# Accumulating the seven products of a Strassen-like group in shared PSUM banks, on one Trainium2 core

## The chip, the core and the metric

The kernel runs on one core of a Trainium2 chip. The engines of the core are named as the profile names them: PE does matrix products (PEld is its loading of weights, which runs beside PE), DVE and ACT are the vector and the scalar engine, POOL and SP mostly issue DMAs here. Each engine works through its own queue in program order and waits on semaphores for the others. Matrix products are written to PSUM, whose banks hold 128 partitions x 512 fp32 values here; DVE and ACT read them there, and DMA moves data between device memory and SBUF. The metric is the device time of one execution in microseconds (us), as the median of several runs.

## The reference

The input `x` has 2048 tokens of 576 channels. The result is `x` plus two branches of the normalised input `xn`: a sliding-window dilated attention (window 8, dilation 2) with its projections, and a mixer with an MLP. The change lies in the MLP:

```python
xn = _layernorm(x, axis=-1)
return x + _A_ref(xn, A_wqkv, A_wo) + _B_ref(xn, B_w1, B_w2, B_w3, B_w4)
...
# in _B_ref, with x1 the result of the token mixing, D = 576, F = 4608
h2 = _gelu(_layernorm(x1, axis=-1) @ w3) @ w4
return x1 + h2
```

All of it is fp32. The kernel reaches that by splitting each operand into a rounded part (fp32r) and a remainder, and multiplying the parts.

## The kernel before

The 4608 hidden columns of the MLP are taken 128 at a time. The first 24 such blocks (12 pairs, `NPL = 12`) go through a plain path: `up` computes a block of `x1 @ w3` for 512 tokens in one PSUM bank, ACT applies the Gelu straight from the bank (`gelu_ps`, lines 783 and 784), `low_part` (line 794) makes the remainder on DVE, and `down` (line 819) multiplies with `w4`.

The last 12 blocks go through the stage that is changed here. It takes a pair of blocks and two blocks of 512 tokens as a 2 x 2 block product, and computes that with seven products of combined operands in place of eight (the Winograd form of Strassen's scheme). A turn of this is a group; there are `NQ = 12` of them, `q = 0` to 11, six for each half of the tokens. The combined operands A11, A12, A22, S1 to S4 (from `w3`) and B11, B21, B22, T1 to T4 (from the tokens) lie ready in SBUF, with signs folded in.

- A product (`product`, line 1056) is seven matmuls (`HALVES`) that accumulate in one bank of 128 x 512 fp32. The banks are named `cc0` to `cc3` and are taken in turn by a count, `nps[1] % 4`. Each of the seven products of a group takes the next.
- The seven products are combined on the way out. ACT copies P1 from its bank into the SBUF buffer Z1 (line 1234). DVE adds the banks of the other six to such buffers (`z_add`, line 1060), P5's bank twice: seven additions a group. They leave c11 in Z4, c22 in Z1, c21 in Z3 and c12 in Z2.
- The Gelu of each of these four is a pair of ACT instructions that read the buffer in SBUF (`gelu_z`, lines 789 and 790): one writes the rounded result to the tile `h`, the other writes the full result back into the buffer. `low_part` then makes the remainder.
- D0 to D7 are eight down projections (`down`), twelve matmuls each, of the hidden values of the group before. Their results go either through ACT (`act.copy` at line 823 into a staging buffer, and a DMA by POOL that adds to device memory, line 824) for the tiles listed in `YD`, or are added to Y by DVE (line 827). Two pairs of banks take turns for them. Of D4 to D7, the last three go through ACT.

The order of the products and down projections of a group is written out by hand: `ORDER = "P1 P2 P6 P5 P7 D0 P4 D1 P3 D2 D3 D4 D5 D6 D7"`, with other orders for groups 0, 1, 5 and 6 (`ORDERS`). In group 6 it begins with `D0 D1 P1 P2`. A `plan` hangs further work behind each of these steps: the splitting of weights (`split_a`, `split_s`, `split_w4`, whose ACT part is line 562) and of token operands (`split_op`, lines 876 to 878 on ACT, after D5 of groups 2 and 3 among others), the combination of weights on DVE (`combine`), DMA loads, and the Gelus of c22 (`gelu22`) and c12 (`gelu12`, at D5 in most groups). The Gelu of c11 follows P5. The Gelu of c21 stands at the start of the next group's code, ahead of its P1, so that on ACT it comes behind the copy of D7. On every engine the instructions stand in the order in which this code issues them.

## Time and profile before

| | |
|---|---|
| timed runs (3) | median 1285.24 us, 1284.25 to 1286.41 |
| span of the profiled execution | 1285.6 us |
| stage with the seven products | about 925 to 1198 us of the span |
| groups, products, down projections in it | 12, 84, 96 |
| PE, DVE, ACT busy in it | 272.6, 202.5 and 146.8 of 273 us |

The profile has of the profiled execution its span; the time that lies around the span isn't shown in it. How to read its lines: in a timeline, the first number is the start in us from the start of the span, the second the busy time in us, then engine, line of the kernel, operation, output `<-` input and shape; brackets hold the idle time of that engine just ahead of the instruction and what ended it. In a list of groups, `x84 | 56.4, 686 | 31.5 <-PE cc L1056 30.9` means 84 instructions, 56.4 us in all, 686 ns each, and 31.5 us idle before them, of which 30.9 ended with that line of PE. In a list of waits, the numbers are the total in us, how often, and the longest.

### The profile page before, as it was taken

What the parts mean: (1) busy time and instruction counts of PE and PEld (TensorE: products, weight loads), DVE (VectorE), ACT (ScalarE), POOL (GpSimd) and SP (SyncE); (2) the same over time, 40 slices, a digit from 0 to 9 for tenths busy, and PEclk for the clock granted to TensorE, in tenths of its full rate; (3) what the DMA queues carried; (4) which work ended last, traced back from release to release, by engine and by line L of the source; (5) the groups of instructions that cost most, each with busy time, mean ns of one, the idle gap of its engine ahead of it and who ended that gap; (6) DMA issues with size and microseconds to landing.
All of it is one profiled execution on the core that took longest, in us unless ns stands there. A gap on an engine that the chain in (4) does not pass through costs nothing.

```text
span 1285.6 us, 19627 instructions
## 1 busy us (share of the span) xinstructions
PE 1271.5 (99%) x7594; PEld 1169.7 (91%) x7594; DVE 950.8 (74%) x1355; ACT 547.0 (43%) x876; POOL 214.3 (17%) x318
## 2 busy tenths in 40 slices
PE   8999999999999999999999999999999999999998
PEld 8999998899898999898989999998899998999998
DVE  6455534677568899999999999967777766887541
ACT  3332125525634434343434343433846567355530
POOL 2011100021221221221211221111112112112200
PEclk9999999999999999999999999999999999999999
DMA  7646784246896887987776867467847787788972
GB/s 205 156 121 138 168 175 140 82 113 194 194 268 147 171 158 200 191 169 151 172 162 144 181 134 164 79 125 179 196 86 128 161 185 150 168 203 188 263 251 83
DMA packets 196173, 210.22 MB, mean 164 GB/s; under 512 B 77920, under 2 KB 134176, under 8 KB 195952
## 3 DMA queue, kind: packets, MB, share of 16 engines
q1 hardware_dynamic: 165536, 144.82, 38.7%
q0 software_dynamic: 30544, 64.16, 31.7%
q8 instruction: 59, 0.97, 0.3%
q14 instruction: 34, 0.28, 0.1%
HBM read 112.98 MB, written 107.28 MB: 171 GB/s over the span
## 4 chain that ended last, share of the span: by engine, by line
PE 78%; issue 7%; DMA 6%; DVE 5%; ACT 2%; POOL 1%; SPq 1%; POOLq 0%; DVEq 0%; ACTq 0%
PE ps L819 26%; PE p L800 21%; PE ps L212 16%; PE cc L1056 6%; PE ps L462 4%; PE ps L309 3%; POOL yd L824 1%; DMA xn<-st 1%; DMA x1n<-xn 1%; DVE L L729 1%; PE ps L477 1%; DMA yd<-ev 1%; SPq L579 1%; DMA yd<-Y 1%; DMA xt<-xn 1%
## 5 line engine op out<-in xcount | busy, mean ns | idle before, releaser
L819 PEld LDWEIGHTS ps<-w,c 128*128 128x128 f32 x3456 | 466.6, 188 | 14.6 <-DVE Y L827 4.0
L819 PE MATMUL ps<-w,c 128*128 128x288 f32 x3456 | 473.1, 294 | 5.6 <-DVE Y L827 2.8
L824 POOL DMA_DIRECT2D yd<-Y x125 | 109.2, 876 | 449.0 <-ACT Y L823 407.7
L823 ACT COPY Y<-ps 128x576 f32<-128x576 f32 x125 | 79.9, 640 | 168.9 <-PE ps L819 86.6
L794 DVE TENSOR_TENSOR c<-Y,c 128x512 fp32r<-128x512 f32 x144 | 98.9, 687 | 59.1 <-ACT Y L784 45.9
L783 ACT ACTIVATE c<-p 128x512 fp32r<-128x512 f32 x96 | 57.6, 600 | 188.9 <-PE p L800 188.9
L212 PE MATMUL ps<-WQ,xt 128*128 128x432 f32 x672 | 134.8, 360 | 0.0
L212 PEld LDWEIGHTS ps<-WQ,xt 128*128 128x128 f32 x672 | 125.6, 188 | 5.7
L726 DVE TENSOR_TENSOR prod<-q,k 128x1152 f32<-128x1152 f32 x64 | 86.6, 1353 | 10.1 <-DMA k<-qkvd 9.4
L827 DVE TENSOR_TENSOR Y<-ps,Y 128x576 f32<-128x576 f32 x108 | 81.2, 752 | 13.5 <-PE ps L819 13.3
L729 DVE TENSOR_REDUCE L<-prod 128x64 f32<-128x1152 f32 x64 | 86.4, 1351 | 1.1
L824 POOL DMA_DIRECT2D yd<-ev x55 | 47.8, 888 | 214.3 <-ACT ev L823 213.2
L800 PE MATMUL p<-xt,w3a 128*128 128x512 f32 x336 | 78.9, 391 | 1.3 <-ACT Y L784 1.3
L1060 DVE TENSOR_TENSOR Y<-cc,Y 128x512 f32<-128x512 f32 x84 | 56.4, 686 | 31.5 <-PE cc L1056 30.9
L800 PE MATMUL p<-xt,w3s 128*128 128x512 f32 x336 | 78.5, 390 | 0.0
L800 PE MATMUL p<-x1n,w3s 128*128 128x512 f32 x336 | 78.5, 390 | 0.0
L800 PE MATMUL p<-x1n,w3a 128*128 128x512 f32 x336 | 78.5, 390 | 0.0
L705 DVE TENSOR_TENSOR prod<-v,L 128x1152 f32<-128x1152 f32 x56 | 75.8, 1354 | 0.8
L709 DVE TENSOR_TENSOR o<-o,prod 128x1152 f32<-128x1152 f32 x56 | 75.8, 1353 | 0.6
L800 PEld LDWEIGHTS p<-xt,w3a 128*128 128x128 f32 x336 | 62.2, 188 | 14.8 <-ACT Y L784 2.1
L119 POOL TENSOR_TENSOR rs<-rs,mhalf 128x1 f32<-128x1 f32 x48 | 30.9, 645 | 261.0 <-DVE rs L118 148.3
L800 PEld LDWEIGHTS p<-xt,w3s 128*128 128x128 f32 x336 | 62.4, 188 | 12.6
(194 smaller groups left out, 1782.1 us busy)
## 6 DMA issues: line engine op xcount, KB each, us to landing
yd<-Y POOLq DMA_DIRECT2D x127, 288.0 KB, 5.3
yd<-ev POOLq DMA_DIRECT2D x55, 288.0 KB, 5.1
Y<-in_B_w_dram SPq DMA_DIRECT2D x23, 576.0 KB, 6.0
w3st<-in_B_w_dram SPq DMA_DIRECT2D x44, 256.0 KB, 6.0
qkvd<-stg SPq DMA_DIRECT2D x24, 432.0 KB, 3.5
xd<-st SPq DMA_DIRECT2D x16, 320.0 KB, 6.0
xd<-big SPq DMA_DIRECT2D x16, 320.0 KB, 7.1
xin<-in_A_x_dram SPq DMA_DIRECT2D x16, 288.0 KB, 3.8
```

Of the source, the lines that this page charges most:

```text
L212: pe.matmul(ps[:, h, :n], xs(a), ws(b, h), start=i == 0, stop=i == len(PAIRS) - 1)
L705: dve.tensor_tensor(dst, vv, Lf[:, :, w:w + 1].to_broadcast([128, TPP * GH, HD]), op=ALU.mult)
L709: dve.tensor_tensor(o, o, dst, op=ALU.add)
L726: dve.tensor_tensor(prod.rearrange("p (j h) d -> p j (h d)", h=GH), q, k[:, r0:r0 + TPP, :], op=ALU.mult)
L729: dve.tensor_reduce(Lf[:, :, w], prod, axis=AX.X, op=ALU.add)
L794: dve.tensor_tensor(h[:, 1, :], g, h[:, 0, :].bitcast(F32), op=ALU.subtract)
L800: pe.matmul(ps, W3[f][:, w, :], x1n[b][:, a, :], start=n == 0, stop=n == len(PAIRS) - 1)
L819: pe.matmul(ps[:, k, :HF], h[:, col], w[:, p, k * HF:(k + 1) * HF], start=n == 0, stop=n == len(seq) - 1)
L823: act.copy(e.rearrange("p (h c) -> p h c", h=2), ps[:, :, :HF])
L824: pool.dma_start(yd[t], e, accum_op=ALU.add)
L827: dve.tensor_tensor(yv, ps[:, :, :HF], yv, op=ALU.add)
L1056: pe.matmul(ps, WX[w][:k, v, SLOT[w], :], area[sb][xk][:k, a, :], start=i == 0, stop=i == len(HALVES) - 1)
```

## The change

Four of the seven products of a group (P1, P6, P7, P4) accumulate in one bank, `ca`, and two (P5, P3) in another, `cc`; P2 has a bank of its own, `cb`. After P1, after P6 and after P7 ACT copies the sum so far from `ca` into Z1, Z2 and Z3 (`keep`). DVE adds P2's bank to Z1, giving c11; P5's bank to Z3, giving c22; and, after P3, the bank with P5 and P3 to Z2, giving c12. With P4 the bank `ca` holds c21, and its Gelu reads it there (`gelu_ps`), writing the full result to Z4. So a group takes three banks in turn where it took seven. Where the sums lie in SBUF changes with it: c11 in Z1, c22 in Z3. `gelu_ps` and `z_add` are not changed.

```diff
-    def product(w, xk):
-        nps[1] += 1
-        ps = qpc.tile([128, 512], F32, name=f"cc{nps[1] % 4}")
+    def product(w, xk, onto=None, last=False):
+        ps = onto
+        if ps is None:
+            nps[1] += 1
+            ps = qpc.tile([128, 512], F32, name=f"cc{nps[1] % 4}")
         for i, (a, v) in enumerate(HALVES):
             k = 128 if a else 96
-            pe.matmul(ps, WX[w][:k, v, SLOT[w], :], area[sb][xk][:k, a, :], start=i == 0, stop=i == len(HALVES) - 1)
+            pe.matmul(ps, WX[w][:k, v, SLOT[w], :], area[sb][xk][:k, a, :],
+                      start=onto is None and i == 0, stop=last and i == len(HALVES) - 1,
+                      skip_group_check=True)
         return ps
+
+    def keep(z, ps):
+        act.copy(by_token(z), in_order(ps))
...
         if q:
-            h21 = gelu_z("c21", Z3)
+            h21 = gelu_ps("c21", ca, Z4)
...
-            hid[q, "c22"] = gelu_z("c22", Z1)
+            hid[q, "c22"] = gelu_z("c22", Z3)
...
-        low22 = lambda: low_part(hid[q, "c22"], Z1)
+        low22 = lambda: low_part(hid[q, "c22"], Z3)
...
             if it == "P1":
-                c1 = product("A11", "B11")
-                act.copy(by_token(Z1), in_order(c1))
+                ca = product("A11", "B11")
+                keep(Z1, ca)
                 if q:
-                    low_part(h21, Z3)
+                    low_part(h21, Z4)
             elif it == "P2":
-                c2 = product("A12", "B21")
-                z_add(Z4, c2, Z1)
+                cb = product("A12", "B21", None, True)
+                z_add(Z1, cb, Z1)
             elif it == "P6":
-                c6 = product("S2", "T2")
-                z_add(Z2, c6, Z1)
+                product("S2", "T2", ca)
+                keep(Z2, ca)
             elif it == "P5":
-                c5 = product("S1", "T1")
-                h11 = hid[q, "c11"] = gelu_z("c11", Z4)
+                cc = product("S1", "T1")
+                h11 = hid[q, "c11"] = gelu_z("c11", Z1)
             elif it == "P7":
-                c7 = product("S3", "T3")
-                z_add(Z3, c7, Z2)
-                z_add(Z1, c5, Z3)
-                z_add(Z2, c5, Z2)
-                low_part(h11, Z4)
+                product("S3", "T3", ca)
+                keep(Z3, ca)
+                z_add(Z3, cc, Z3)
+                low_part(h11, Z1)
             elif it == "P4":
-                c4 = product("A22", "T4")
-                z_add(Z3, c4, Z3)
+                product("A22", "T4", ca, True)
             elif it == "P3":
-                c3 = product("S4", "B22")
-                z_add(Z2, c3, Z2)
+                product("S4", "B22", cc, True)
+                z_add(Z2, cc, Z2)
...
-    h21 = gelu_z("c21", Z3)
+    h21 = gelu_ps("c21", ca, Z4)
...
-            low_part(h21, Z3)
+            low_part(h21, Z4)
```

## The prediction

> **What bounds the kernel now.** I read the page's busy shares first, then the stage that holds all the edits, then the matrix engine's waits in it, and last the two engines that gain and lose work, in order of time.

> ```profile
> span 1285.6 us, 19627 instructions
> PE 1271.5 (99%) x7594; PEld 1169.7 (91%) x7594; DVE 950.8 (74%) x1355; ACT 547.0 (43%) x876; POOL 214.3 (17%) x318
> 925.00:1198.00 273.00, 272.64 (x1622) 247.22 (x1621) 202.48 (x340) 146.84 (x230) 46.91 (x55) 1.00 0.75 163
> PE ps L819 <- ACT ev L823: 0.4, 1, 0.4
> ```

> The third line is one stretch of the busy-time-by-stretches view: the seven-product stage, 273 us of twelve groups, with the busy time of PE, PEld, DVE, ACT and POOL, then the granted clock (1.00). The fourth is the whole list of PE's waits in that stretch: a single one of 0.4 us. So in this stage PE alone sets the time, DVE is idle a quarter of it and ACT almost half. An edit can gain at most about that one gap (0.4 us, and below 1 us with its restart); it can lose as much as it makes PE wait.

> One group in PE's timeline (start, busy us, instructions):

> ```profile
> 1111.85 3.40 PE L1056 MATMUL cc<-x1n,w3a 128*128 128x512 f32 x14
> 1115.09 3.39 PE L1056 MATMUL cc<-xt,w3s 128*128 128x512 f32 x14
> 1118.31 1.77 PE L1056 MATMUL cc<-x1n,w3s 128*128 128x512 f32 x7
> 1119.92 1.75 PE L819 MATMUL ps<-w,c 128*128 128x288 f32 x12
> 1121.51 1.78 PE L1056 MATMUL cc<-xt,w3a 128*128 128x512 f32 x7
> ```

> P1 and P2 stand in the first row, P6 and P5 in the second, then P7, D0 and P4. From start to start a product takes (1115.09 - 1111.85) / 2 = 1.62 us and a down projection 1.59 us. A row's busy time runs some 0.16 us past the next row's start, because matmuls overlap.

> **What the change removes and adds, off the path.** The matmuls are the same in number and shape and PE's order of products and downs is unchanged; no DMA is added, removed or moved on any queue.

> ```profile
> L1060 DVE TENSOR_TENSOR Y<-cc,Y 128x512 f32<-128x512 f32 x84 | 56.4, 686 | 31.5 <-PE cc L1056 30.9
> L1234 ACT COPY Y<-cc 128x512 f32<-128x512 f32 x12 | 6.8, 570 | 1.0 <-PE cc L1056 1.0
> ```

> DVE loses four of seven additions a group: 12 x 4 x 0.686 = 33 us of its 202. ACT gains two copies a group: 12 x 2 x 0.570 = 14 us on its 147. Both still lie under PE's 273, and PE never waited for DVE here, so the 33 us are worth nothing.

> **New waits inside a group.** P6, P7 and P4 now write the bank that ACT has just copied out, so each must wait for the copy before it. The second copy, for one, starts about 0.1 us after P6's last matmul, which ends 1.78 us after P6 starts; with 0.57 us and 0.05 us of signalling P7 is free 2.5 us after P6's start, and PE wants it only at 2 x 1.62 = 3.24, since P5 stands between. P4 has D0 between: 1.62 + 1.59 = 3.21 against 2.5. P3 writes onto the bank that DVE reads after the third copy: 2.5 + 0.1 + 0.69 = 3.3 against 6.4 from P7's start, or 4.8 in the groups with fewer downs between. Cover is 0.7 us where it is thinnest; without it the loss would be 0.19 us and more each time (restart, below). The Gelus that read the sums get them no later than before: c11 still after P2's addition, c22 after a copy and one addition where it had two additions, c12 after P3's. All this holds where ACT is not late, and in the middle of a group it has holes (first row, 7.55 us). Only in group 0 it is late, behind operand splits (second and third row):

> ```profile
> 1124.93 0.64 ACT L823 COPY ev<-ps 128x576 f32<-128x576 f32 x1 [7.55 <-PE ps L819]
> 929.29 0.58 ACT L1234 COPY Y<-cc 128x512 f32<-128x512 f32 x1
> 929.96 3.40 PE L1056 MATMUL cc<-xt,w3s 128*128 128x512 f32 x14
> ```

> The copy ends at 929.87 and P6 starts at 929.96, its weight load a little earlier: I book 0.15 us, bounds 0 and 0.3.

> **The new wait at the boundary of groups.** Here is the cost. Seven banks a group were taken in turn from four; now three are. Group g takes the counts 3g+1 (four products), 3g+2 (P2) and 3g+3; the next group's P2 takes 3g+5, which modulo 4 is 3g+1: the bank in which group g's c21 stands. Formerly c21 was finished into SBUF by DVE and its Gelu read that; now the Gelu pair reads the bank itself, and it stands in ACT's queue where it always stood, behind D7's copy. So P2 must wait for the end of that pair, and all of PE's queue with it; nobody then waits for P2 but work that itself has slack. ACT at the same boundary:

> ```profile
> 1108.88 0.64 ACT L823 COPY ev<-ps 128x576 f32<-128x576 f32 x1 [1.34 <-PE ps L819]
> 1111.14 1.16 ACT L562 CAST w<-Y 128x1152 fp32r<-128x1152 f32 x1
> 1112.19 0.64 ACT L823 COPY ev<-ps 128x576 f32<-128x576 f32 x1
> 1112.72 0.64 ACT L789 ACTIVATE c<-Y 128x512 fp32r<-128x512 f32 x1
> 1113.40 0.63 ACT L790 ACTIVATE Y<-Y 128x512 f32<-128x512 f32 x1
> 1113.93 0.57 ACT L1234 COPY Y<-cc 128x512 f32<-128x512 f32 x1
> ```

> D5's copy waited for PE (1.34 us), then ACT is busy without a hole: Gelu of c12, D6's copy, the w4 cast, D7's copy, and at 1112.72 and 1113.40 the pair in question. P2 would start at 1111.85 + 1.62 = 1113.47, before the pair's end. How long the pair takes from a PSUM bank shows in the stage before, where the same two activations read one:

> ```profile
> 902.65 0.60 ACT L783 ACTIVATE c<-p 128x512 fp32r<-128x512 f32 x1 [2.53 <-PE p L800]
> 903.14 0.59 ACT L784 ACTIVATE Y<-p 128x512 f32<-128x512 f32 x1
> ```

> 1.08 us from the first start to the second end, against 1.31 above from SBUF. So P2 is released at 1112.72 + 1.08 + 0.05 = 1113.85, 0.38 us late. [...]

> Two boundaries, into groups 3 and 4, have an operand split (three activations) in ACT's chain after D5:

> ```profile
> 1013.56 1.04 ACT L876 ACTIVATE xt<-xt 128x1024 fp32r<-128x1024 f32 x1
> 1015.82 0.62 ACT L823 COPY ev<-ps 128x576 f32<-128x576 f32 x1
> 1017.92 0.64 ACT L789 ACTIVATE c<-Y 128x512 fp32r<-128x512 f32 x1
> 1014.80 3.40 PE L1056 MATMUL cc<-x1n,w3a 128*128 128x512 f32 x14
> 993.93 0.64 ACT L789 ACTIVATE c<-Y 128x512 fp32r<-128x512 f32 x1
> 990.81 3.40 PE L1056 MATMUL cc<-x1n,w3a 128*128 128x512 f32 x14
> ```

> The split pushes D6's copy out by 1015.82 - 1013.56 = 2.26 us. P2 is wanted at 1014.80 + 1.62 = 1016.42 and released at 1017.92 + 1.13 = 1019.05: 2.63 us late. The other one: 993.93 + 1.13 - 992.43 = 2.63.

> Of the other eight (into groups 1, 2, 5, 7 to 11) the first and the last:

> ```profile
> 943.54 0.63 ACT L789 ACTIVATE c<-Y 128x512 fp32r<-128x512 f32 x1
> 942.80 3.40 PE L1056 MATMUL cc<-x1n,w3a 128*128 128x512 f32 x14
> 1184.79 0.64 ACT L789 ACTIVATE c<-Y 128x512 fp32r<-128x512 f32 x1
> 1183.91 3.40 PE L1056 MATMUL cc<-x1n,w3a 128*128 128x512 f32 x14
> ```

> 944.67 against 944.42 is 0.25, 1185.92 against 1185.53 is 0.39. Done the same way, the eight are 0.25 twice and 0.37 to 0.39 six times: 2.8 us. Into group 6 there is none: two downs stand between the pair and P1.

> **What a stop costs beside its length.** The one wait of this kind that the stage has:

> ```profile
> 1061.32 0.62 ACT L823 COPY ev<-ps 128x576 f32<-128x576 f32 x1
> 1061.99 4.92 PEld L819 LDWEIGHTS ps<-w,c 128*128 128x128 f32 x36 [0.59 <-ACT ev L823]
> 1061.99 5.16 PE L819 MATMUL ps<-w,c 128*128 128x288 f32 x36 [0.36 <-ACT ev L823]
> 1066.99 3.39 PE L1056 MATMUL cc<-x1n,w3a 128*128 128x512 f32 x14
> 1083.07 4.92 PE L819 MATMUL ps<-w,c 128*128 128x288 f32 x36
> 1087.83 3.40 PE L1056 MATMUL cc<-x1n,w3a 128*128 128x512 f32 x14
> ```

> The copy ends at 1061.94 and PE goes on at 1061.99 (the 0.05 used above), but its three downs take 1066.99 - 1061.99 = 5.00 us, against 1087.83 - 1083.07 = 4.76 without a stop. The weight load, too, restarts only at the release, and is no longer under a matmul. Lower bound 0, upper 0.24; I take 0.19 (the page has 188 ns for a load), ten times: 1.9 us. [...] The row has the load waiting.

> **Sum.** 2 x 2.63 + 2.8 + 1.9 + 0.15 = 10.1 us. PE is saturated, so none of it is made up later, and ACT's chain at each boundary is tied to D5's end on PE, so the lateness repeats unchanged. The profiled span of 1285.6 lies 0.4 us above the median of the timed runs, 1285.24; the span would be 1295.7, and the time 1285.24 + 10.1 = 1295.3.

> **The rivals.**
> Not slower: DVE's 33 us bring ACT's chain forward, so the pair ends before P2 wants the bank. Then P2 costs nothing and at best the stage's one gap goes: 1285.24 - 0.6 (0.36 idle, 0.24 restart) = 1284.6. It decides once the pair ends 0.6 us earlier at eight boundaries and 2.8 at two. For it: ACT does wait for DVE's additions in places.

> ```profile
> L789 ACT ACTIVATE c<-Y 128x512 fp32r<-128x512 f32 x48 | 30.4, 634 | 15.1 <-DVE Y L1060 15.1
> 1214.13 1.85 PE L819 MATMUL ps<-w,c 128*128 128x288 f32 x12 [1.28 <-ACT Y L823]
> ```

> The first row has these 15.1 us. Against: the chain that sets the pair starts from PE's D5, not from DVE. 5%.
> Only the long stalls: the short ones (0.25 to 0.39 us) vanish if ACT runs a little tighter, as with a copy less at the boundary. 2 x (2.63 + 0.19) = 5.6, so 1290.9. Against: six instructions in a row there have no hole. 9%.
> Later gaps swallow part: the 0.6 us gap at 1061.99 and the 1.28 us one at 1214.13 (row above) close if their cause, DMA landings say, does not shift with PE: 1295.3 - 1.9 = 1293.4. Against: the first hangs on ACT work behind D1's copy, which shifts too. 8%.
> Weight loads run ahead: the load under a waiting matmul is done by the time it is released, so a stop costs its length alone, 10.1 - 1.9 = 8.2 and 1293.4. For it: loads do overlap matmuls everywhere else. Against: PEld's row at 1061.99, and the 5.00 us for three downs. 10%. [...]
> The in-group waits bite: if waiting products lose the weight load's cover even where the copy is in time, 36 waits x 0.19 = 6.8 more: 1302.1. Against: PE's rows show an even 1.62 us although products waited for older readers of their banks before. 8%.

> **How the numbers follow.** The forecast has 60%. Its own range: restarts 0 to 0.24 (8.2 to 10.6), pair 0.1 us shorter or longer at ten boundaries (1 us), so 1292.5 to 1297. The range is widened to the cheaper rivals and part of the way to the dearer one: 1290.5 to 1299. About 0.2% (2.6 us) is what a measurement can tell from no change. Only the first rival is not slower: 2% faster, 4% the same, 94% slower; the point over its 5% is for causes that I don't see.

> **What would show it.** PE's waits in the stage should list P2 (the products' line) waiting for the second Gelu, ten times, two of them near 2.5 us, with the weight load waiting alongside; DVE busy about 33 us less, ACT about 11 to 14 us more; P6, P7, P4 and P3 with no waits except perhaps group 0. I would be wrong if P1 and P2 stay 1.62 us apart at the boundaries, if the copies appear among PE's waits, or if PE's granted clock falls after the long stalls.

## The result and the profile after

The median of five runs is 1297.14 us (1294.95 to 1300.15), against 1286.41 us (1284.25 to 1287.11, five runs) for the kernel before, measured beside it: a ratio of 1.0091 [1.0078, 1.0104], slower by 10.7 us. Ratios here and below are estimated from the single runs, with a 95% interval; the quotient of two medians differs a little (1.0083 here). The profiled execution took 1297.46 us, its span is 10.1 us longer than before's.

The page of the kernel after (its span and busy shares), then the row of the seven-product stage in the busy-time-by-stretches view (length, then PE, PEld, DVE, ACT, POOL busy, then the granted clock):

```profile
span 1295.7 us, 19586 instructions
PE 1274.2 (98%) x7594; PEld 1168.2 (90%) x7594; DVE 921.3 (71%) x1307; ACT 558.4 (43%) x900; POOL 214.4 (17%) x318
925.00:1208.00 283.00, 276.17 (x1624) 246.58 (x1623) 173.45 (x293) 158.02 (x254) 47.43 (x55) 1.00 0.74 157
```

DVE has 48 instructions and 29.5 us less, ACT 24 instructions and 11.4 us more, PE the same 7594 matmuls. DVE was relieved as intended, and the kernel got slower: the stage is 10 us longer, and PE, busy for 272.6 of 273 us before, now is for 276.2 of 283. The granted clock is 1.00 in both. So the new time is time in which PE stands.

The kernel after: PE's waits in the stage, then those of its weight loads (what waits, for what, total us, times, longest):

```profile
PE cc L1058 <- ACT Y L784: 6.3, 8, 2.5
PE ps L819 <- ACT ev L823: 0.4, 1, 0.4
```

```profile
PEld cc L1058 <- ACT Y L784: 10.8, 10, 2.9
```

Line 784 is the second activation of the Gelu that reads PSUM, the last reader of the bank with c21; line 1058 is the products' line. The weight load is held as often as there are boundaries with a shared bank, ten times; of PE itself only eight waits show: into groups 1 and 7, where the wait is short, the modelled end of the last matmul covers it. The 0.4 us was there before.

PE's timeline of the kernel after at three boundaries, into group 2, into group 3 and into group 8, from P1 on (start, busy us; in brackets the idle time ahead):

```profile
967.81 1.79 PE L1058 MATMUL cc<-x1n,w3a 128*128 128x512 f32 x7
969.82 1.87 PE L1058 MATMUL cc<-x1n,w3a 128*128 128x512 f32 x7 [0.23 <-ACT Y L784]
971.53 3.39 PE L1058 MATMUL cc<-xt,w3s 128*128 128x512 f32 x14
...
992.29 1.79 PE L1058 MATMUL cc<-x1n,w3a 128*128 128x512 f32 x7
996.53 1.86 PE L1058 MATMUL cc<-x1n,w3a 128*128 128x512 f32 x7 [2.46 <-ACT Y L784]
998.23 3.39 PE L1058 MATMUL cc<-xt,w3s 128*128 128x512 f32 x14
...
1119.72 1.79 PE L1058 MATMUL cc<-x1n,w3a 128*128 128x512 f32 x7
1121.74 1.91 PE L1058 MATMUL cc<-x1n,w3a 128*128 128x512 f32 x7 [0.23 <-ACT Y L784]
1123.49 3.45 PE L1058 MATMUL cc<-xt,w3s 128*128 128x512 f32 x14
1126.79 1.80 PE L1058 MATMUL cc<-x1n,w3s 128*128 128x512 f32 x7
```

P1 and P2 shared one row before; now a wait parts them. The bracket understates the loss, because a busy time runs past the next start: what counts is start to start. From P1 to P6 it is 3.72 us into group 2, 5.94 into group 3 and 3.77 into group 8, against 3.24 before.

ACT's timeline of the kernel after at the boundary into group 3:

```profile
991.05 1.04 ACT L876 ACTIVATE xt<-xt 128x1024 fp32r<-128x1024 f32 x1
...
993.30 0.62 ACT L823 COPY ev<-ps 128x576 f32<-128x576 f32 x1
993.82 1.15 ACT L562 CAST w<-Y 128x1152 fp32r<-128x1152 f32 x1
994.87 0.63 ACT L823 COPY ev<-ps 128x576 f32<-128x576 f32 x1
995.40 0.59 ACT L783 ACTIVATE c<-cc 128x512 fp32r<-128x512 f32 x1
995.89 0.58 ACT L784 ACTIVATE Y<-cc 128x512 f32<-128x512 f32 x1
996.37 0.58 ACT L1064 COPY Y<-cc 128x512 f32<-128x512 f32 x1
```

There is no hole: operand split, D6's copy, the w4 cast, D7's copy, then the pair, 1.07 us from 995.40 to 996.47, and P2 starts at 996.53. Behind it stands the copy after P1 (line 1064), which ends at 996.95; that row matters in the first experiment.

### The profile page after: what moved, and what is told of

Same layout as the page of the kernel before. It is cut to its first block, busy times and chain, and to the rows that moved or that the text cites. A ratio compares the mean times of both kernels' runs of the same rounds, so it can differ in the third digit from the quotient of the medians.

```text
span 1295.7 us, 19586 instructions
## 1 busy us (share of the span) xinstructions
PE 1274.2 (98%) x7594; PEld 1168.2 (90%) x7594; DVE 921.3 (71%) x1307; ACT 558.4 (43%) x900; POOL 214.4 (17%) x318
## 5 line engine op out<-in xcount | busy, mean ns | idle before, releaser
L819 PEld LDWEIGHTS ps<-w,c 128*128 128x128 f32 x3456 | 466.6, 188 | 15.0 <-DVE Y L827 4.7
L819 PE MATMUL ps<-w,c 128*128 128x288 f32 x3456 | 473.1, 294 | 6.1 <-DVE Y L827 3.5
L823 ACT COPY Y<-ps 128x576 f32<-128x576 f32 x125 | 79.9, 640 | 162.6 <-PE ps L819 80.9
L783 ACT ACTIVATE c<-p 128x512 fp32r<-128x512 f32 x96 | 57.6, 600 | 190.8 <-PE p L800 190.8
L726 DVE TENSOR_TENSOR prod<-q,k 128x1152 f32<-128x1152 f32 x64 | 86.6, 1353 | 11.1 <-DMA k<-qkvd 10.4
L800 PE MATMUL p<-xt,w3a 128*128 128x512 f32 x336 | 79.0, 391 | 1.4 <-ACT Y L784 1.4
L800 PE MATMUL p<-xt,w3s 128*128 128x512 f32 x336 | 78.6, 390 | 0.0
L800 PE MATMUL p<-x1n,w3a 128*128 128x512 f32 x336 | 78.5, 390 | 0.0
L800 PE MATMUL p<-x1n,w3s 128*128 128x512 f32 x336 | 78.5, 390 | 0.0
L800 PEld LDWEIGHTS p<-xt,w3a 128*128 128x128 f32 x336 | 62.2, 188 | 14.9 <-ACT Y L784 2.2
L800 PEld LDWEIGHTS p<-xt,w3s 128*128 128x128 f32 x336 | 62.4, 188 | 12.6
L800 PEld LDWEIGHTS p<-x1n,w3a 128*128 128x128 f32 x336 | 62.4, 188 | 12.6
```

The source lines that it names most:

```text
L726: dve.tensor_tensor(prod.rearrange("p (j h) d -> p j (h d)", h=GH), q, k[:, r0:r0 + TPP, :], op=ALU.mult)
L800: pe.matmul(ps, W3[f][:, w, :], x1n[b][:, a, :], start=n == 0, stop=n == len(PAIRS) - 1)
L819: pe.matmul(ps[:, k, :HF], h[:, col], w[:, p, k * HF:(k + 1) * HF], start=n == 0, stop=n == len(seq) - 1)
L823: act.copy(e.rearrange("p (h c) -> p h c", h=2), ps[:, :, :HF])
```

## The experiments

Theory A is that of the prediction: P2's bank is still being read, by a Gelu pair that is late on ACT. Rivals: B, the cost lies in the products that go on in a bank that ACT has just copied (P6, P7, P4, P3); C, it lies in the clock or in the matmuls themselves. A stage's length below is from the start of group 0's P1 to the first down projection behind group 11's P4 and P3: 273.27 us before (925.14 to 1198.41), 283.14 after (925.67 to 1208.81).

**Other banks, so that no product starts in the bank with c21.** Two banks for `ca` in turn, one for P2, one for P5 and P3; everything else is that of the change.

```diff
-    def product(w, xk, onto=None, last=False):
+    def product(w, xk, onto=None, last=False, bank=0):
...
-            nps[1] += 1
-            ps = qpc.tile([128, 512], F32, name=f"cc{nps[1] % 4}")
+            ps = qpc.tile([128, 512], F32, name=f"cc{bank}")
...
-                ca = product("A11", "B11")
+                ca = product("A11", "B11", bank=q % 2)
...
-                cb = product("A12", "B21", None, True)
+                cb = product("A12", "B21", None, True, 2)
...
-                cc = product("S1", "T1")
+                cc = product("S1", "T1", bank=3)
```

> The changed kernel, but P2 always writes bank cc2, P5 and P3 always cc3, and the accumulating bank alternates between cc0 and cc1 from group to group; nothing else. Theory (P2 waits at the boundary of groups for the Gelu pair that reads c21 from its bank): no P2 waits any more, and 9 to 9.5 us of the 10.1 us in the span go, so that the time is within 1 us of the kernel before (ratio 0.9995 to 1.001). Rival (the products that write onto a bank that ACT or DVE has just read, P6, P7, P4 and P3, lose the time): these waits are all still there, so the time stays 9 to 11 us above the kernel before (ratio 1.007 to 1.009). Rival (part of the loss is that accumulating is slower by itself): the time stays in between, and the products last longer than 1.62 us from start to start.

1288.64 us (11 runs) against 1285.72, ratio 1.0021 [1.0012, 1.003]; stage 276.65 us. Of 9.9 us of stage 6.5 are gone, 3.4 stay. PE's waits, PE's rows and ACT's rows of this kernel at the boundary into group 3:

```profile
PE cc L1057 <- ACT Y L1063: 2.6, 2, 1.3
```

```profile
989.21 3.40 PE L1057 MATMUL cc<-x1n,w3a 128*128 128x512 f32 x14
993.93 3.50 PE L1057 MATMUL cc<-xt,w3s 128*128 128x512 f32 x14 [1.32 <-ACT Y L1063]
```

```profile
992.82 0.59 ACT L784 ACTIVATE Y<-cc 128x512 f32<-128x512 f32 x1
993.30 0.58 ACT L1063 COPY Y<-cc 128x512 f32<-128x512 f32 x1
```

P1 and P2 are one row of 14 again: P2 waits nowhere. But into groups 3 and 4 P6 now waits for the copy after P1, which stands behind the late pair: it ends at 993.88, P6 starts at 993.93 and not at 989.21 + 3.24 = 992.45, 1.48 us late, twice. In the kernel after, P2's stop had hidden this one (copy done at 996.95, P6 at 998.23). So A holds for the short stops, and the long ones had a second wait behind the first, which the expectation missed.

**The sum copied out after P4, Gelu from SBUF as before.** This frees c21's bank early and keeps the three banks in turn.

```diff
-            h21 = gelu_ps("c21", ca, Z4)
+            h21 = gelu_z("c21", Z4)
...
                 product("A22", "T4", ca, True)
+                keep(Z4, ca)
```

> The changed kernel with its own banks in turn, but after P4 ACT copies the finished c21 to Z4, and the Gelu of c21 reads Z4 in SBUF as it did before the change: one copy a group more on ACT (0.57 us), the bank free some 18 us earlier. Theory (the reader of the bank is late, not the taking of banks in turn as such): no P2 waits, time within 1 us of the kernel before although ACT does 12 copies more than in the changed kernel. Rival (ACT is simply too full, or in-group waits): 10 us or more above the kernel before.

1291.05 us (5 runs), ratio 1.0034 [1.0021, 1.0047]; stage 277.06 us. Its only waits of products:

```profile
PE cc L1058 <- ACT Y L1064: 3.1, 2, 1.5
```

P2 is free here too, without another bank, so the bank's reader was the cause and not the choice of bank. The same two P6 are left, 0.2 us later than with other banks, as the pair from SBUF is 0.2 us longer (995.36 to 996.65 here, 1.29 us, against 992.33 to 993.41, 1.08 us, with other banks). The time missed the expectation: it is 5.3 us above the kernel before, of which the stage explains 3.8. One piece of the rest shows in the profiled execution ahead of the stage, where no edit reaches: group 0's P1 starts at 926.42 us, against 925.14 before. PE's longest wait for DVE at line 827 was 2.2 us in it, against 1.4 before, and its mean clock was 0.999.

**The operand split away from the boundary.** The splits behind D5 of groups 2 and 3 go behind D0 of groups 3 and 4; the banks stay those of the change.

```diff
         if q in (2, 3):
             k = ("T4", "B22")[q - 2]
             at("P2", get_op, 1, k)
-            at("D5", split_op, 1, k)
+        if q in (3, 4):
+            at("D0", split_op, 1, ("T4", "B22")[q - 3])
```

> The changed kernel with the two operand splits that followed D5 in groups 2 and 3 (three ACT instructions, two on DVE each) put behind D0 of groups 3 and 4, where ACT is idle for about 4 us. Theory (a stop is as long as ACT's chain from D5's copy to the end of the Gelu pair is too long): the two stops of 2.6 us become like the others (0.37 us late and 0.1 for the restart), 2 x 2.2 = 4.5 us less than the changed kernel, about 5.5 us above the kernel before (ratio 1.0035 to 1.0055), still ten waits on PE's weight load list, none longer than 0.7 us. Rival (each stop costs a fixed restart, whatever its length): no change against the changed kernel.

1290.15 us (5 runs), ratio 1.0039 [1.0026, 1.0053]; stage 278.75 us, 4.4 less than after. PE's waits, and the boundary into group 3:

```profile
PE cc L1058 <- ACT Y L784: 1.8, 8, 0.2
```

```profile
993.05 1.79 PE L1058 MATMUL cc<-x1n,w3a 128*128 128x512 f32 x7
995.07 1.87 PE L1058 MATMUL cc<-x1n,w3a 128*128 128x512 f32 x7 [0.23 <-ACT Y L784]
996.78 3.39 PE L1058 MATMUL cc<-xt,w3s 128*128 128x512 f32 x14
```

The long stops have become short ones. So what made the two long is the split, as A has it; the rival, a fixed restart whatever the length, would have left the stage as it was.

**The cover inside the group taken away.** Other banks as above, and P6 ahead of P2, so that it follows the P1 whose sum ACT must copy first (the weight splits behind P2 and P6 change places with them, except in group 1).

```diff
-    ORDER = "P1 P2 P6 P5 P7 D0 P4 D1 P3 D2 D3 D4 D5 D6 D7"
+    ORDER = "P1 P6 P2 P5 P7 D0 P4 D1 P3 D2 D3 D4 D5 D6 D7"
```

> As the first kernel of this set (own banks, no wait of P2), but in eight groups (2 to 4 and 7 to 11) P6 comes right behind P1 and P2 after it, with the ACT part of the weight split that followed P2 now behind P6. P6 then wants the bank 1.62 us after P1's start, while the first copy out of it ends 0.48 us after the Gelu pair. Theory (the waits inside a group cost nothing only because a product stands between): P6 waits eight times, 0.85 us in six groups, 3.1 us in groups 3 and 4, with restarts 12 us more than the first kernel of this set and about 12 us above the kernel before (ratio 1.008 to 1.011). Rival (a wait on the copy is free, or the copies run ahead of need by more than the distance shows): no more than 2 us above the first kernel of this set.

1302.29 us (4 runs), ratio 1.0129 [1.011, 1.0148]; stage 287.77 us, 11.1 more than with other banks alone; the median is 13.7 us more, where 12 were expected. PE's waits, and its rows at the boundaries into groups 3 and 4:

```profile
PE cc L1057 <- ACT Y L1063: 10.1, 8, 2.9
```

```profile
995.70 3.24 PE L1057 MATMUL cc<-xt,w3s 128*128 128x512 f32 x7 [2.93 <-ACT Y L1063]
998.74 2.02 PE L1057 MATMUL cc<-x1n,w3a 128*128 128x512 f32 x7
...
1024.46 1.87 PE L1057 MATMUL cc<-xt,w3s 128*128 128x512 f32 x7 [2.93 <-ACT Y L1063]
1026.17 1.77 PE L1057 MATMUL cc<-x1n,w3a 128*128 128x512 f32 x7
```

The six ordinary groups lose 0.68 or 0.70 us of idle time each by the trace, the two long ones 2.93. So B is a real cost, and in the change it is the order of the products that hides it. The rows show something else: after the first stop of 2.93 us seven matmuls take 3.04 us to the next start, after the second 1.71. In stretches of one microsecond behind each stop (the last three numbers: granted clock, DMA share, GB/s):

```profile
997.00:998.00 1.00, 1.00 (x4) 0.77 (x3) 0.00 (x0) 0.00 (x0) 0.00 (x0) 0.50 0.58 90
...
1025.00:1026.00 1.00, 1.00 (x6) 0.81 (x5) 0.00 (x0) 0.00 (x0) 0.00 (x0) 1.00 1.03 113
```

The clock was 0.50 behind the first stop and 1.00 behind the second. So C exists, behind one of the two long stops. Of the 11.1 us some 1.6 are that: 1.33 on these seven matmuls and 0.24 on the next seven (1.86 us by their starts for 1.62). The four timed runs go with the mean clock: 1300.28 and 1300.54 at 0.999, 1304.05 at 0.996, 1305.76 at 0.995.

**Both repairs together**: other banks and the split away from the boundary.

> Own banks (as in e1) and the two operand splits early (as in e3) together. In e1 two stops were left, where P6 waited 1.5 us for the first copy, which stands behind the Gelu pair that the split had pushed out. Theory (ACT's chain after D5 is what is late at those two boundaries, whoever waits for it): no product waits any more, the stage from group 0's P1 to the first down of the tail is 273.3 to 273.7 us as in the kernel before (273.3), the time is the same as before within 0.1%. Rival (part of what e1 still lost, 2.9 us in the times, comes from other work that the change adds, ACT's copies for one): 2 us or more above the kernel before.

1286.00 us (11 runs) against 1285.96 (21 runs), ratio 1.0005 [0.9996, 1.0014]; stage 273.32 us, 0.05 from before. No product waits any more; the one wait of PE left in the stage is the old one:

```profile
PE ps L819 <- ACT ev L823: 0.4, 1, 0.4
```

The two causes make up the whole loss of the stage. Singly the repairs took 6.5 and 4.4 us off it, together 9.8, for at the two long boundaries both act on the same stop. And this kernel still has the 48 additions less: DVE's relief is worth nothing that shows.

**The last gap.** On top of both repairs, the split of T2 in group 5 goes from behind D4 to behind D6, so that ACT comes sooner to the copy that this gap waits for.

```diff
-            at("D4", split_op, 1, "T2")
...
             at("D6", low12)
+            at("D6", split_op, 1, "T2")
```

> e5, and in group 5 the split of operand T2 moved on ACT and DVE from D4 to D6, ahead of its use in group 6. In the kernel before, PE has its one gap of the stage there: D7 waits for D5's copy, which stands behind that split. Theory (the same chain on ACT): the gap at the end of group 5 goes and the stage is 0.8 to 1.0 us shorter than in e5, about 272.5 us; in the times about 0.1% under the kernel before, at the limit of what can be told. Rival (the gap is DMA-bound): unchanged against e5.

1286.18 us (11 runs), ratio 1.0001 [0.9992, 1.001]; stage 273.17 us. The expected gain did not come: the wait moved two down projections on, to the last one ahead of group 6's P1. There it waits for the copy of D7, which now stands on ACT behind the moved split.

```profile
1065.00 1.85 PE L819 MATMUL ps<-w,c 128*128 128x288 f32 x12 [0.34 <-ACT ev L823]
```

No version here beats the kernel before by more than a measurement can tell.

**Stops of four lengths, in both orders.** Is it a stop's length that lets the clock fall, or its place? The kernel after, with 2, 3, 4 and 5 extra copies of 128x512 on ACT (of scratch, unused) ahead of the Gelu pair at the boundaries into groups 8, 9, 10 and 11; then with 5, 4, 3 and 2.

```diff
         if q:
+            for _ in range({8: 2, 9: 3, 10: 4, 11: 5}.get(q, 0)):
+                act.copy(RT, RT)
             h21 = gelu_ps("c21", ca, Z4)
```

> The changed kernel with 2, 3, 4 and 5 more ACT copies of 128x512 within a scratch buffer (0.65 us each) ahead of the Gelu pair of c21 at the boundaries into groups 8, 9, 10 and 11, so that P2's stops there get longer: PE idle about 1.5, 2.1, 2.8 and 3.5 us; the two long stops of 2.46 us stay. Their length alone adds 14 x 0.65 = 9 us to the changed kernel. Theory (a stop of nearly 3 us lets the granted clock fall to half, as after one stop of 2.93 us in e4, where seven matmuls took 3.0 us in place of 1.6): after some of the stops of 2.5 us and more, hardly after those under 2, PE runs at a granted clock of 0.50 for about 3.4 us, which costs some 1.6 us each: 10 to 16 us above the changed kernel, mean clock 0.994 to 0.998. Rival (that event had nothing to do with the stop): clock 1.00 behind all six stops, 9 us.

> As e7, with 5, 4, 3 and 2 more copies at the same four boundaries in turn, so that length and place are told apart: by the theory the granted clock falls behind the stops of about 3 us and more, now those into groups 8 and 9, by the rival nowhere; a fall behind groups 10 and 11 again would tie it to the place.

1309.12 us (4 runs), ratio 1.0178 [1.0159, 1.0197], and 1306.14 us (4 runs), ratio 1.0161 [1.0147, 1.0175]. Against the kernel after's 1297.14 these are 12.0 and 9.0 us more; the theory had 10 to 16 and the rival 9, so the medians don't tell the two apart. The traces do. P2 at the four boundaries, first with the stops growing, then with them shrinking:

```profile
1124.56 1.90 PE L1058 MATMUL cc<-x1n,w3a 128*128 128x512 f32 x7 [1.39 <-ACT Y L784]
1151.01 1.89 PE L1058 MATMUL cc<-x1n,w3a 128*128 128x512 f32 x7 [2.04 <-ACT Y L784]
1177.99 3.35 PE L1058 MATMUL cc<-x1n,w3a 128*128 128x512 f32 x7 [2.69 <-ACT Y L784]
1208.42 3.23 PE L1058 MATMUL cc<-x1n,w3a 128*128 128x512 f32 x7 [3.34 <-ACT Y L784]
```

```profile
1122.62 3.35 PE L1058 MATMUL cc<-x1n,w3a 128*128 128x512 f32 x7 [3.34 <-ACT Y L784]
1152.46 3.16 PE L1058 MATMUL cc<-x1n,w3a 128*128 128x512 f32 x7 [2.69 <-ACT Y L784]
1180.46 1.89 PE L1058 MATMUL cc<-x1n,w3a 128*128 128x512 f32 x7 [2.04 <-ACT Y L784]
1206.14 1.90 PE L1058 MATMUL cc<-x1n,w3a 128*128 128x512 f32 x7 [1.39 <-ACT Y L784]
```

P2's busy time tells the clock: about 1.9 us at full clock, 3.2 to 3.4 at half. In these two executions it goes with the stop's length in either order: behind 2.69 and 3.34 us the clock was half, behind 1.39 and 2.04 it wasn't. The two stops of 2.46 us that the kernel after has anyway, into groups 3 and 4, are there in both kernels; in each, the first was followed by half clock and the second not, so length is not all (last section). The kernel with growing stops:

```profile
996.82 3.22 PE L1058 MATMUL cc<-x1n,w3a 128*128 128x512 f32 x7 [2.46 <-ACT Y L784]
...
1024.87 1.91 PE L1058 MATMUL cc<-x1n,w3a 128*128 128x512 f32 x7 [2.46 <-ACT Y L784]
```

## Why the prediction was right

Its sum was 10.1 us; the span grew by 10.1, of which the stage has 9.87, the time ahead of it 0.53 and the time behind it -0.30. That the span agrees to the tenth is luck: group 0's P1 starts anywhere from 922.00 to 926.42 us in the ten profiled executions, though no edit touches the work before it. The test is the stage's 9.87. Term by term, with the measured side read as the growth of P1 to P6 over 3.24 us (to D0 where that comes earlier, in group 1):

| term of the sum | predicted | measured |
|---|---|---|
| two long stops, with restart | 2 x (2.63 + 0.19) = 5.64 | 2 x 2.70 = 5.40 |
| eight short stops, with restart | 2.8 + 8 x 0.19 = 4.3 | 0.34 + 2 x 0.48 + 0.39 + 4 x 0.53 = 3.8, and 0.1 in each of groups 7 to 11 on the products behind = 4.3 |
| P6 of group 0 | 0.15 | 0.12, over P6, P5 and P7; no wait is recorded there |

- **Off the path.** Held. The additions' group fell from 56.4 to 24.9 us, by 31.5 for the 33 booked, and ACT gained 11.4 of the 11 to 14; with both repairs this relief left the time where it was (ratio 1.0005).
- **The wait at the boundary.** Held in place, cause and number: ten held weight loads. P2 starts 969.82 - 967.81 - 1.62 = 0.39 us late into group 2, 996.53 - 992.29 - 1.62 = 2.62 into group 3, 0.40 into group 8, against 0.37 to 0.39 and 2.63. That the split makes the long ones was shown by moving it, that the reader of the bank makes all of them by the two kernels that free the bank.
- **The pair from PSUM.** Booked at 1.08 us from the stage before; 1.07 into group 3.
- **The restart.** Right in kind, a little high in size up to group 5: 998.23 - 996.53 = 1.70 for P2 where 1.62 is usual, so 0.08, and 0.09 into group 2, against 0.19. From group 7 on it is 0.13 in P2 (1123.49 - 1121.74 = 1.75) and 0.1 spread over the next products (P6 and P5 take 3.30 for 3.23), 0.23. Where P2's start can be read it was never 0, and the weight loads were held with it (10.8 us in PEld's list), so the rival by which weight loads run ahead of a wait fell. Why the two halves of the stage differ was not tried.
- **In-group waits.** True of the kernel as it is: no copy is among PE's waits. But the reason given, at least 0.7 us of cover where ACT is not late and lateness in group 0 alone, was wrong at the two long boundaries. There ACT is late for the copy after P1 as well, by 1.48 us, and only P2's stop hid it. The sum was not touched, since the two waits lie side by side; each of the first two repairs was overrated by this step.
- **The rivals.** Not slower and only the long stalls fell: the short stops came, eight of them. Later gaps swallowing part came true in a small way: the gap of 0.4 us stayed, the one of 1.28 us in the tail became 0.93, and the 0.35 us between these account for the -0.30 above. The in-group waits did not bite: 6.8 us more would not fit in the stage's 9.87.
- **The median.** 1297.14 is 1.8 us above the predicted 1295.3. Of this 1.2 us are the kernel before, 1286.41 beside these runs and 1285.24 in the runs the prediction started from. For the remaining 0.6 us a clock that falls after the long stalls, the condition named in the prediction, is a possible cause: the profiled execution kept 1.00 in the stage, but three of the five timed runs had a mean clock of 0.997 or 0.998, and 0.002 x 1296, an estimate of the loss at 0.998, is 2.6 us. It isn't shown. Those runs have no trace, and one of them, 1296.68 at 0.998, took less than the 1297.46 at 1.000.

## What to carry to other kernels

When accumulators are shared or renamed, list for each bank its next writer and its last reader, and place the reader in its engine's queue: a sum that another engine reads in place keeps its bank until that engine has worked off all that stands before it (here P2 started at 996.53 us, behind a pair that ended at 996.47). Here, with the engine that sets the time busy for 272.6 of 273 us, taking 48 additions off another one bought nothing that shows (ratio 1.0005), and the waits that it newly met cost their length and a restart (0.08 to 0.23 us), and behind some of the longer ones a spell of half clock (1.3 us on seven matmuls; next section). And a wait can hide another: before a repair is priced, work out who else is late on the same queue once the first wait is gone.

## What was unexpected of the hardware

Some stops of PE of 2.46 to 3.34 us were followed by half clock. In the stage, over the kernels with the products' stops, recorded idle times of 2.04 us and less were never followed by it; of 2.46 us in two of six cases, of 2.69 in both, of 2.93 in one of two, of 3.34 in both. Stretches of the kernel with growing stops (length, PE's busy time, and so on; granted clock third from the end):

```profile
992.92:996.33 3.41, 1.44 (x7) 0.83 (x5) 3.13 (x4) 3.38 (x7) 0.99 (x2) 1.00 0.61 76
996.33:999.74 3.41, 2.92 (x7) 2.35 (x8) 1.01 (x2) 2.05 (x4) 0.72 (x1) 0.50 0.91 112
1020.22:1023.64 3.42, 2.19 (x12) 1.53 (x10) 2.90 (x4) 3.37 (x6) 0.85 (x1) 1.00 0.53 79
1023.64:1027.05 3.41, 2.18 (x9) 1.81 (x10) 1.92 (x3) 2.79 (x6) 0.87 (x1) 1.00 0.90 109
1177.23:1184.06 6.83, 6.07 (x14) 4.79 (x15) 2.80 (x4) 2.32 (x5) 0.00 (x0) 0.50 1.08 302
1207.95:1211.37 3.42, 2.95 (x7) 2.38 (x8) 0.69 (x1) 0.89 (x2) 0.00 (x0) 0.50 0.89 164
```

A spell of two steps followed the stop of 2.69 us when the stops grew and that of 3.34 us when they shrank, so the longer stop did not go with the longer spell. In the kernel without cover one step of half clock made the same seven matmuls 1.3 us dearer than the same stop without it (3.04 against 1.71).
